# A six-layer cross network on one core: x0's first rows in three transfers, turned tile by tile; bias products with 128 rows; another order of ACT's last y

## The chip, the cores and the metric

The kernel runs on one core of a Trainium2 chip. The metric is the device time of one execution in microseconds. Engines are named as in the profile: PE (TensorE), DVE (VectorE), ACT (ScalarE), POOL (GpSimd), SP (SyncE, which here only issues DMAs).

## The reference

```python
B, F, D, L = 4096, 26, 16, 6
Din = min(F * D, 1024)            # 416
# x0 (B, Din), ws (L, Din, Din), bs (L, Din), all bfloat16
def reference(x0, ws, bs):
    x = x0
    for l in range(ws.shape[0]):
        x = x0 * (x @ ws[l] + bs[l]) + x
    return x
```

## The kernel before

The kernel works on x transposed: columns of x are partitions, rows of x run along the free axis. The 416 columns are three chunks c (or k, as the contracted side) of 128 and a tail of 32. The 4096 rows are four pairs p of two blocks of 512 rows. Since x stays a product with x0, only t = x @ w + (running sum of the biases) is kept in PSUM: PSUM accumulates over the layers of one pair, and each layer's x is (PSUM + cb) * x0, where `cb_sb` holds the running sums of the biases plus one. One step n = p * 6 + l is one layer of one pair, 24 in all.

A step on PE is `main(p, l, 0, n)` (block 0, chunks m = 0 to 2), `tail(p, l, n)` (the tail's share, four row groups side by side, and the tail's own output in `ps_tail`), and `main(p, l, 1, n)`. Each of the five results (tail products, tail output, chunks 0 to 2 of block 1) raises `s_pe`. DVE answers with six scalar_tensor_tensor per step (`s_dve`): chunk 0 of block 0, the tail, chunk 1 of block 0, chunks 0 to 2 of block 1. ACT and POOL make chunk 2 of block 0 together (L702, L289), and ACT copies the tail's halves into each other's partitions (L666).

In the first step block 0 is done by `first()` instead. x0's first 512 rows come as rows into `xin_sb` (four tiles j of 128 rows), PE transposes them into PSUM (L320) against `ident`, and DVE copies them to `x0T_sb` (L579), raising `s_ev`. Chunk 0 is copied in two halves (j 0 to 1, j 2 to 3, in different PSUM banks), chunks 1 and 2 in one piece each. Then three groups of products follow, for k = 0, 1, 2 (L348, shown as L380, the helper's line); group k waits for its weights `s_w0[k]` and for `s_ev` >= k + 2. Between k = 0 and k = 1 PE transposes the tail of both blocks (L352) from `xtn_sb`, which POOL puts together from `xin_sb` and `xtb_sb` (L260), and makes the running sums of the biases with four products (L331): `bsa_sb` (a row of ones and six rows of biases) and `bs4_sb` (the tail's 32 biases four times, made by POOL at L269) against the triangle `u_sb`. DVE turns these into `cb_sb` (L589); POOL then makes `cl_sb` (L279).

Step 0's `tail` waits for `s_ev` 5 (the tail of x0), `s_cb`, `s_w30` (the tail rows of layer 0's weights, `w3_sb`, spread from 32 to 128 partitions by two ACT copies, L674), `s_dup` (the tail's halves swapped by DVE, L587) and `s_wc0` (the corner of the weights, four POOL copies, L276).

Ahead of all that PE runs 28 products of constants, `idle(28)` (L308), whose results are not used.

Issue order of the DMAs at the start. SP's queue: x0 rows 0 to 255, three weight chunks of layer 0 (L165), a transposing DMA for block 1 (L168), then, after a wait for the last of the three weights, the weights of layers 1 to 5 (L173, L177). ACT's queue: x0 rows 256 to 511 (L643), the 32 tail columns of block 1 (`xtb_sb`, L646), the biases (L649), the tail rows of layer 0's weights (L650). Behind these on ACT stand the load of its table and a dummy activation (L653).

The last step (n = 23) is done the other way round by `last()`: the outputs are rows, so that no transpose is needed. Eight row tiles j get three products each with x as the stationary side (`rows`, L489), the tail's products (L551), and the sum so far, y, added in by products with the identity (`add_y`, L498). y is PSUM plus `cl_sb`, copied by ACT in `sums` (L681) after step 22 in the order of a list of (block, chunk, steps of DVE to wait for), each raising `s_y`; chunk 3 is the tail's `yt_sb`. DVE makes one y too (L621, `s_yd`). `rows(j)` waits for `s_y` at 2, 3, 3, 4 for j = 0 to 3, L551 for `s_y` 6 and `s_yd`. In step 22's `main` of block 1, chunk 2, the second half waits for `s_y` 1, as its bank also holds the tail that ACT reads. DVE (L630, L636) and ACT with POOL (L723, L297) then multiply by x0's rows, and SP and ACT send the tiles out.

Of the kernel before, what the change touches and what calls it, by code (L numbers as in the profile page):

```python
# [11 lines left out]
def bass_standalone__dcn_v2_cross__recsys_kernel(  # L12
# [13 lines left out]
    B, D = x0.shape  # L26
    L = ws.shape[0]
    DF = 384
    DR = D - DF
    assert DR == 32  # L30
    NB = 512
# [8 lines left out]
    with ExitStack() as es:  # L40
# [25 lines left out]
        ones_sb = sb("ones_sb", [128, 128])  # L66
        bsa_sb = sb("bsa_sb", [L + 1, D])
        bs4_sb = sb("bs4_sb", [L + 1, 4, DR])
        u_sb = sb("u_sb", [L + 1, L])
        cb_sb = sb("cb_sb", [128, 4, L], FP32)  # L70
# [28 lines left out]
        def sem(name):  # L99
            return es.enter_context(nc.semaphore(name))  # L100
# [6 lines left out]
        s_w = [sem("s_w%d" % i) for i in range(L)]  # L107
        s_xin = [sem("s_xin%d" % i) for i in range(2)]
        s_xtb, s_xtp, s_inT, s_ev = sem("s_xtb"), sem("s_xtp"), sem("s_inT"), sem("s_ev")
# [43 lines left out]

        DH = D // 2
        MADE = ((2, 0, D), (3, 0, DH))
# [3 lines left out]
        def _(sp):  # L159

            sp.dma_start(
                xin_sb[:, 0:2, :], x0[0:256, :].rearrange("(j b) d -> b j d", b=128)
            ).then_inc(s_xin[0], 16)
            for k in range(3):
                sp.dma_start(  # L165
                    w_sb[:, 0, k, :], ws[0, k * 128:(k + 1) * 128, :]
                ).then_inc(s_w0[k], 16)
# [75 lines left out]
        def _(pool):  # L243
            pool.memset(ones_sb[:, :], 1.0).then_inc(s_ones, 1)
            pool.memset(bsa_sb[0:1, :], 1.0).then_inc(s_setup, 1)
            pool.wait_ge(s_ones, 1)
# [4 lines left out]
            pool.affine_select(  # L251
                out=u_sb[:, :], in_=ones_sb[0:L + 1, 0:L], pattern=[[1, L]],
                compare_op=ALU.is_ge, fill=0.0, base=1, channel_multiplier=-1,
# [3 lines left out]
            for h, src in enumerate((xin_sb[:, :, DF:D], xtb_sb[:, :, :])):  # L257
# [11 lines left out]
            pool.tensor_copy(  # L269
                out=bs4_sb[:, :, :], in_=bsa_sb[:, DF:D].unsqueeze(1).broadcast_to([L + 1, 4, DR])  # L270
            ).then_inc(s_bs4, 1)
# [31 lines left out]
        def _(pe):  # L303
# [5 lines left out]

            idle(28)  # L310
            pe.wait_ge(s_setup, 3)
# [3 lines left out]

            def turn(c):
                for j in range(4):
                    if c == 0 and j % 2 == 0:
                        pe.wait_ge(s_xin[j // 2], 16)
                    ins = pe.transpose(  # L320
                        out=psT[:, at(c, j), j * 128:(j + 1) * 128],
                        in_=xin_sb[:, j, c * 128:(c + 1) * 128], identity=ident[:, :],
                    )
                    if c == 0 and j == 1:
                        ins.then_inc(s_inT, 1)
                ins.then_inc(s_inT, 1)

# [11 lines left out]
            def first():  # L339

                for c in range(3):
                    turn(c)
                for k in range(3):
# [5 lines left out]
                    if k == 0:  # L349
                        pe.wait_ge(s_xtp, 2)  # L350
                        for c in range(2):
                            ins = pe.transpose(  # L352
                                out=psT[:, 2, c * 128:(c + 1) * 128],
                                in_=xtn_sb[:, 0, c, :], identity=ident[:, :],
                            )
                        ins.then_inc(s_inT, 1)
                        biases()

# [37 lines left out]
            def main(p, l, blk, n):  # L396
                for m in range(3):
# [12 lines left out]
                    if blk == 1 and m == 2 and n == N1 - 1:  # L410

                        for h in range(2):
                            if h == 1:
                                pe.wait_ge(s_y, 1)
                            for k in range(3):
# [21 lines left out]
            def tail(p, l, n):  # L437
                if n == 0:
                    pe.wait_ge(s_ev, 5)
                    pe.wait_ge(s_cb, 1)  # L440
                    pe.wait_ge(s_w30, 2)
                    pe.wait_ge(s_wt[0], 16)
# [133 lines left out]
        def _(dve):  # L576
# [9 lines left out]
            for o, i in swapped(x0t_sb[:, 0]):  # L586
                dve.tensor_copy(out=o, in_=i).then_inc(s_dup, 1)  # L587
            dve.wait_ge(s_inT, 6)
            dve.tensor_copy(  # L589
# [52 lines left out]
        def _(act):  # L642
            act.dma_start(  # L643
                xin_sb[:, 2:4, :], x0[256:512, :].rearrange("(j b) d -> b j d", b=128)
            ).then_inc(s_xin[1], 16)
            act.dma_start(  # L646
                xtb_sb[:, :, :], x0[NB:2 * NB, DF:D].rearrange("(j b) d -> b j d", b=128)
            ).then_inc(s_xtb, 16)
            act.dma_start(bsa_sb[1:L + 1, :], bs[:, :]).then_inc(s_bs, 16)  # L649
            act.dma_start(w3_sb[0:DR, 0, :], ws[0, DF:D, :]).then_inc(s_wt[0], 16)  # L650

# [17 lines left out]
            act.wait_ge(s_wt[0], 16)  # L669
            for i in range(2):  # L670
                r = DR << i
                if i:
                    act.wait_ge(s_w30, i)
                act.activation(  # L674
                    out=w3_sb[r:2 * r, 0, :], in_=w3_sb[0:r, 0, :], func=ACTF.Copy
                ).then_inc(s_w30, 1)

            def sums(n):
# [6 lines left out]
                act.wait_ge(s_cl, 1)  # L685
                for blk, c, d in ((0, 3, 2), (0, 0, 2), (0, 2, 2), (0, 1, 3), (1, 0, 4), (1, 1, 5)):
                    act.wait_ge(s_dve, DV * n + d)
# [72 lines left out]
```

## Time and profile before

| what | value |
|---|---|
| time, median of 3 runs | 129.14 us (129.0 to 129.2) |
| time of the profiled execution | 129.91 us |
| its span, first to last instruction | 128.1 us |
| PE busy | 124.6 us, 97% of the span |
| DVE / ACT / POOL busy | 93.2 / 45.3 / 32.0 us |
| chain that ended last | PE 95%, DVE 3% |
| granted clock over the span | 1.00 |

All times in the text come from the profiled execution and count from its first instruction. PE is also shown as PEld, its weight loads, which overlap its products; a product's duration includes some 0.2 us of draining, while the next one starts in the meantime, so the spacing of starts tells the pace. A DMA's time to landing counts from the start of its issue.

### The profile page before, as it was taken

Reading aid. Unit: us, or ns where it says so; the run is one execution under the profiler, and the core shown is the slowest. Engines: PE = TensorE matmul, PEld = TensorE weight load, DVE = VectorE, ACT = ScalarE, POOL = GpSimd, SP = SyncE. Lnnn points to the kernel's source line nnn. Section 1 sums busy time; section 2 is a strip of 40 time slices with the busy share of each in tenths; the row PEclk is TensorE's granted clock in tenths of the full one; section 3 lists DMA queues with packets and bytes.
Section 4 is the critical chain, followed back from the end, with each engine's and each line's share of the span. In section 5 each row is a group of like instructions: output and inputs, shape, how many; then the busy total and the mean of one; then the engine's idle time right before and its main releaser. Section 6 shows DMA issues by size and latency. Waiting matters only on the chain.

```text
span 128.1 us, 5809 instructions
## 1 busy us (share of the span) xinstructions
PE 124.6 (97%) x2931; PEld 66.3 (52%) x2403; DVE 93.2 (73%) x155; ACT 45.3 (35%) x99; POOL 32.0 (25%) x42
## 2 busy tenths in 40 slices
PE   7999999999999999999999999999999999999991
PEld 7654554555445545545545545545545545545571
DVE  0449669669669669679678688697696696696873
ACT  0435436436404314214314224224224134134820
POOL 5323303303303213213123023033033033033040
PEclk9999999999999999999999999999999999999999
DMA  3979999397399700697100987000000758000017
GB/s 97 265 167 299 199 126 158 52 109 157 75 284 71 146 12 15 131 121 237 35 15 10 96 160 262 9 0 5 0 15 15 139 112 266 5 5 0 0 49 222
DMA packets 35624, 13.27 MB, mean 104 GB/s; under 512 B 26987, under 2 KB 35601, under 8 KB 35601
## 3 DMA queue, kind: packets, MB, share of 16 engines
q1 hardware_dynamic: 33912, 12.07, 49.0%
q10 hardware_dynamic: 1688, 0.83, 2.4%
q8 instruction: 21, 0.34, 1.2%
q14 instruction: 3, 0.02, 0.0%
HBM read 3.99 MB, written 3.41 MB: 58 GB/s over the span
## 4 chain that ended last, share of the span: by engine, by line
PE 95%; DVE 3%; DVEq 0%; issue 0%
PE ps L390 61%; PE ps L370 11%; PE ps L457 8%; PE ps L478 6%; PE ps L380 4%; PE ps L308 2%; DVE o_sb L630 2%; PE ps L320 1%; PE ps L551 0%; DVE o_sb L636 0%; PE ps L352 0%; PE ps L331 0%; DVEq L40 0%; DVEq L627 0%
## 5 line engine op out<-in xcount | busy, mean ns | idle before, releaser
L601 DVE SCALAR_TENSOR_TENSOR xT_sb<-ps,cb_sb,x0T_sb 128x512 bf16<-128x512 f32 x100 | 69.4, 744 | 22.3 <-PE ps L457 22.3
L390 PE MATMUL ps<-xT_sb,w_sb 128*32 128x512 bf16 (+1 forms) x1380 | 75.7, 343 | 0.0
L390 PEld LDWEIGHTS ps<-xT_sb,w_sb 128*32 128x32 bf16 x1380 | 37.0, 97 | 35.2 <-issue 8.1
L289 POOL TENSOR_TENSOR xT_sb<-t_sb,x0T_sb 128x512 bf16<-128x512 f32 x20 | 23.2, 1162 | 72.3 <-ACT t_sb L702 72.3
L702 ACT ACTIVATE t_sb<-ps,cb_sb 128x512 f32<-128x512 f32 x23 | 15.8, 687 | 61.1 <-PE ps L457 61.1
L370 PE MATMUL ps<-xT_sb,w_sb 128*32 128x256 bf16 x444 | 26.6, 273 | 0.0
L666 ACT ACTIVATE xt_sb<-xt_sb 64x256 bf16<-64x256 bf16 x38 | 15.8, 415 | 9.8 <-DVE xt_sb L610 9.3
L390 PE MATMUL ps<-x0T_sb,w_sb 128*32 128x512 bf16 (+1 forms) x252 | 14.1, 344 | 0.0
L601 DVE SCALAR_TENSOR_TENSOR xo_sb<-ps,cb_sb,x0T_sb 128x512 bf16<-128x512 f32 x15 | 10.4, 744 | 3.3 <-PE ps L457 3.3
L390 PEld LDWEIGHTS ps<-x0T_sb,w_sb 128*32 128x32 bf16 x252 | 6.7, 97 | 6.5 <-issue 1.5
L457 PE MATMUL ps<-xt_sb,w_sb 32*128 32x256 bf16 x228 | 9.6, 271 | 0.0
L478 PE MATMUL ps<-xT_sb,w_sb 128*32 128x256 bf16 x228 | 9.5, 273 | 0.0
L610 DVE SCALAR_TENSOR_TENSOR xt_sb<-ps,cb_sb,x0t_sb 128x256 bf16<-128x256 f32 x20 | 9.5, 475 | 0.0
L457 PEld LDWEIGHTS ps<-xt_sb,w_sb 32*128 32x128 bf16 x228 | 4.2, 92 | 6.2 <-issue 6.1
L289 POOL TENSOR_TENSOR xo_sb<-t_sb,x0T_sb 128x512 bf16<-128x512 f32 x3 | 3.5, 1163 | 11.2 <-ACT t_sb L702 11.2
L478 PEld LDWEIGHTS ps<-xT_sb,w_sb 128*32 128x32 bf16 x228 | 6.1, 97 | 0.1
L390 PE MATMUL ps<-xt_sb,wc_sb 128*32 128x256 bf16 x76 | 5.6, 283 | 0.0
L380 PE MATMUL ps<-w_sb,xT_sb 128*128 128x416 bf16 (+2 forms) x27 | 5.2, 320 | 0.0
L370 PE MATMUL ps<-x0T_sb,w_sb 128*32 128x256 bf16 x84 | 5.0, 273 | 0.0
L660 ACT ACTIVATE wc_sb<-w_sb 32x32 bf16<-32x32 bf16 x20 | 4.5, 226 | 0.5
L579 DVE COPY x0T_sb<-ps 128x256 bf16<-128x256 bf16 (+1 forms) x4 | 1.4, 358 | 4.5 <-PE ps L320 4.4
L390 PEld LDWEIGHTS ps<-xt_sb,wc_sb 128*32 128x32 bf16 x76 | 1.9, 92 | 4.0 <-issue 4.0
(54 smaller groups left out, 51.3 us busy)
## 6 DMA issues: line engine op xcount, KB each, us to landing
out_dram<-o_sb SPq DMA_DIRECT2D x3, 832.0 KB, 4.2
w_sb<-in_ws_dram SPq DMA_DIRECT2D x5, 312.0 KB, 5.3
xr_sb<-in_x_dram SPq DMA_DIRECT2D x1, 832.0 KB, 6.2
w_sb<-in_ws_dram SPq DMA_DIRECT2D x5, 104.0 KB, 3.4
out_dram<-o_sb SPq DMA_DIRECT2D x2, 208.0 KB, 2.1
w_sb<-in_ws_dram ACTq DMA_DIRECT2D x3, 104.0 KB
xin_sb<-in_x_dram SPq DMA_DIRECT2D x1, 208.0 KB, 3.1
xin_sb<-in_x_dram ACTq DMA_DIRECT2D x1, 208.0 KB, 3.3
```

What stands on the lines that cost most here:

```text
L289: pool.tensor_tensor(out=xdst(p, l, 0, 2), in0=t_sb[:, n % 2, :], in1=x0c(p, 0, 2), op=ALU.mult,).then_inc(s_pl, 1)
L308: pe.matmul(ps[:, 0, 0:128], lhsT=ones, rhs=ones, start=True, stop=True)
L370: return pe.add_instruction(mybir.InstMatmult(name="I-%d" % (1000000 + count[0]), engine=mybir.EngineType.PE, start_tensor_calc=start, sto ...
L380: return pe.matmul(out, lhsT=lhsT, rhs=rhs, start=start, stop=stop, skip_group_check=True)
L390: ins = pe.matmul(out[c:c + 32, :], lhsT=lhsT[:, c:c + 32], rhs=rhs, start=start, stop=stop, skip_group_check=True, tile_position=(0, c),)
L457: ins = pe.matmul(part(blk, m, h ^ other), lhsT=w3_sb[32 * g:32 * g + 32, l, m * 128:(m + 1) * 128], rhs=xt[32 * g:32 * g + 32, other, :], ...
L478: ins = pe.matmul(ps_tail[32 * g:32 * g + 32, :], lhsT=w_sb[:, l, k, DF:D], rhs=xsrc(p, l, g % 2, k)[:, (g // 2) * NT:(g // 2 + 1) * NT], ...
L601: dve.scalar_tensor_tensor(out=halves(xdst(p, l, blk, c)), in0=chunk2(blk, c), scalar=cb_sb[:, c, l:l + 1], in1=halves(x0c(p, blk, c)), op ...
L610: dve.scalar_tensor_tensor(out=tdst(p, l), in0=ps_tail, scalar=cb_sb[:, 3, l:l + 1], in1=x0t_sb[:, p, 0, :], op0=ALU.add, op1=ALU.mult,).t ...
L660: act.activation(out=wc_sb[gs, l, gs], in_=w3_sb[gs, l, DF:D], func=ACTF.Copy).then_inc(s_wc, 1)
L666: act.activation(out=o, in_=i, func=ACTF.Copy).then_inc(s_dup, 1)
L702: act.activation(out=halves(t_sb[:, n % 2, :]), in_=chunk2(0, 2), func=ACTF.Identity, bias=cb_sb[:, 2, l:l + 1],).then_inc(s_act, 1)
```

## The change

- x0's first 512 rows come in three transfers: tile 0 (SP's first), tile 1 (ACT's first), tiles 2 and 3 (SP's second). Layer 0's first weight chunk goes to ACT's queue as its second; SP keeps the other two. On ACT the tail weights go ahead of the biases, and the biases wait for the memset of `bsa_sb`.
- PE transposes all three chunks of tile 0, then of tile 1, then tiles 2 and 3 chunk by chunk. 23 filler products instead of 28.
- The bias products take 128 rows: `bsa_sb`, `bs4_sb` and `u_sb` have 128 partitions (ones, and zeros in `u_sb` below row 6), and the products come between k = 1 and k = 2.
- The second copy that spreads `w3_sb` is split: ACT takes the left half of the columns, DVE the right half, ahead of its copy of the bias sums. `tail` waits for three copies.
- ACT's y for chunk 0 of block 0 comes first, after DVE's first step, and the tail's second; PE's wait in step 22 is for two y.

```diff
--- before.py
+++ after.py
@@ -27,6 +27,7 @@
     L = ws.shape[0]
     DF = 384
     DR = D - DF
+    DH = D // 2
     assert DR == 32
     NB = 512
     NP = B // (2 * NB)
@@ -64,9 +65,10 @@
         act_sb = sb("act_sb", [128, 1], FP32)
         ident = sb("ident", [128, 128])
         ones_sb = sb("ones_sb", [128, 128])
-        bsa_sb = sb("bsa_sb", [L + 1, D])
-        bs4_sb = sb("bs4_sb", [L + 1, 4, DR])
-        u_sb = sb("u_sb", [L + 1, L])
+
+        bsa_sb = sb("bsa_sb", [128, D])
+        bs4_sb = sb("bs4_sb", [128, 4, DR])
+        u_sb = sb("u_sb", [128, L])
         cb_sb = sb("cb_sb", [128, 4, L], FP32)
         ps = es.enter_context(nc.psum_tensor("ps", [128, 8, NB], FP32))
         psT = ps.bitcast(BF16)
@@ -105,7 +107,7 @@
         s_wt = [sem("s_wt%d" % i) for i in range(L)]
         s_w0 = [sem("s_w0_%d" % i) for i in range(3)]
         s_w = [sem("s_w%d" % i) for i in range(L)]
-        s_xin = [sem("s_xin%d" % i) for i in range(2)]
+        s_xin = [sem("s_xin%d" % i) for i in range(3)]
         s_xtb, s_xtp, s_inT, s_ev = sem("s_xtb"), sem("s_xtp"), sem("s_inT"), sem("s_ev")
         s_x0 = [sem("s_x0_%d" % i) for i in range(NP)]
         s_tn = [sem("s_tn%d" % i) for i in range(NP)]
@@ -151,17 +153,17 @@
 
         DB = D - (NB - D)
 
-        DH = D // 2
         MADE = ((2, 0, D), (3, 0, DH))
         SPLIT = ((ps[:, 7, 0:DB], 0, DB), (ps[:, 6, D:NB], DB, D))
 
         @block.sync
         def _(sp):
 
+            sp.dma_start(xin_sb[:, 0, :], x0[0:128, :]).then_inc(s_xin[0], 16)
             sp.dma_start(
-                xin_sb[:, 0:2, :], x0[0:256, :].rearrange("(j b) d -> b j d", b=128)
-            ).then_inc(s_xin[0], 16)
-            for k in range(3):
+                xin_sb[:, 2:4, :], x0[256:512, :].rearrange("(j b) d -> b j d", b=128)
+            ).then_inc(s_xin[2], 16)
+            for k in (1, 2):
                 sp.dma_start(
                     w_sb[:, 0, k, :], ws[0, k * 128:(k + 1) * 128, :]
                 ).then_inc(s_w0[k], 16)
@@ -242,14 +244,14 @@
         @block.gpsimd
         def _(pool):
             pool.memset(ones_sb[:, :], 1.0).then_inc(s_ones, 1)
-            pool.memset(bsa_sb[0:1, :], 1.0).then_inc(s_setup, 1)
+            pool.memset(bsa_sb[:, :], 1.0).then_inc(s_setup, 1)
             pool.wait_ge(s_ones, 1)
             pool.affine_select(
                 out=ident[:, :], in_=ones_sb[:, :], pattern=[[-1, 128]],
                 compare_op=ALU.is_equal, fill=0.0, base=0, channel_multiplier=1,
             ).then_inc(s_setup, 1)
             pool.affine_select(
-                out=u_sb[:, :], in_=ones_sb[0:L + 1, 0:L], pattern=[[1, L]],
+                out=u_sb[:, :], in_=ones_sb[:, 0:L], pattern=[[1, L]],
                 compare_op=ALU.is_ge, fill=0.0, base=1, channel_multiplier=-1,
             ).then_inc(s_setup, 1)
             pool.memset(wc_sb[:, :, :], 0.0).then_inc(s_g, 1)
@@ -267,7 +269,7 @@
             pool.wait_ge(s_bs, 16)
             pool.wait_ge(s_setup, 1)
             pool.tensor_copy(
-                out=bs4_sb[:, :, :], in_=bsa_sb[:, DF:D].unsqueeze(1).broadcast_to([L + 1, 4, DR])
+                out=bs4_sb[:, :, :], in_=bsa_sb[:, DF:D].unsqueeze(1).broadcast_to([128, 4, DR])
             ).then_inc(s_bs4, 1)
             pool.wait_ge(s_g, 1)
             pool.wait_ge(s_wt[0], 16)
@@ -307,23 +309,25 @@
                 for _ in range(n):
                     pe.matmul(ps[:, 0, 0:128], lhsT=ones, rhs=ones, start=True, stop=True)
 
-            idle(28)
+            idle(23)
             pe.wait_ge(s_setup, 3)
             def at(c, j):
 
                 return 4 if (c, j // 2) == (0, 1) else (2, 3, 6)[c]
 
-            def turn(c):
-                for j in range(4):
-                    if c == 0 and j % 2 == 0:
-                        pe.wait_ge(s_xin[j // 2], 16)
+            def turns():
+
+                order = [(j, c) for j in range(2) for c in range(3)]
+                order += [(j, c) for c in range(3) for j in range(2, 4)]
+                for j, c in order:
+                    if c == 0 and j < 3:
+                        pe.wait_ge(s_xin[j], 16)
                     ins = pe.transpose(
                         out=psT[:, at(c, j), j * 128:(j + 1) * 128],
                         in_=xin_sb[:, j, c * 128:(c + 1) * 128], identity=ident[:, :],
                     )
-                    if c == 0 and j == 1:
+                    if (j, c) == (1, 0) or j == 3:
                         ins.then_inc(s_inT, 1)
-                ins.then_inc(s_inT, 1)
 
             def biases():
                 pe.wait_ge(s_bs4, 1)
@@ -338,8 +342,7 @@
 
             def first():
 
-                for c in range(3):
-                    turn(c)
+                turns()
                 for k in range(3):
                     pe.wait_ge(s_w0[k], 16)
                     pe.wait_ge(s_ev, k + 2)
@@ -354,6 +357,7 @@
                                 in_=xtn_sb[:, 0, c, :], identity=ident[:, :],
                             )
                         ins.then_inc(s_inT, 1)
+                    elif k == 1:
                         biases()
 
             def pieces(blk, m, x):
@@ -411,7 +415,7 @@
 
                         for h in range(2):
                             if h == 1:
-                                pe.wait_ge(s_y, 1)
+                                pe.wait_ge(s_y, 2)
                             for k in range(3):
                                 o, rhs = pieces(blk, m, xsrc(p, l, blk, k))[h]
                                 ins = columns(
@@ -438,7 +442,7 @@
                 if n == 0:
                     pe.wait_ge(s_ev, 5)
                     pe.wait_ge(s_cb, 1)
-                    pe.wait_ge(s_w30, 2)
+                    pe.wait_ge(s_w30, 3)
                     pe.wait_ge(s_wt[0], 16)
                 elif l == 0:
                     pe.wait_ge(s_x0t[p], 16)
@@ -585,6 +589,10 @@
             dve.wait_ge(s_ev, 5)
             for o, i in swapped(x0t_sb[:, 0]):
                 dve.tensor_copy(out=o, in_=i).then_inc(s_dup, 1)
+            dve.wait_ge(s_w30, 1)
+            dve.tensor_copy(
+                out=w3_sb[64:128, 0, DH:D], in_=w3_sb[0:64, 0, DH:D]
+            ).then_inc(s_w30, 1)
             dve.wait_ge(s_inT, 6)
             dve.tensor_copy(
                 out=cb_sb[:, :, :],
@@ -640,14 +648,14 @@
 
         @block.scalar
         def _(act):
-            act.dma_start(
-                xin_sb[:, 2:4, :], x0[256:512, :].rearrange("(j b) d -> b j d", b=128)
-            ).then_inc(s_xin[1], 16)
+            act.dma_start(xin_sb[:, 1, :], x0[128:256, :]).then_inc(s_xin[1], 16)
+            act.dma_start(w_sb[:, 0, 0, :], ws[0, 0:128, :]).then_inc(s_w0[0], 16)
             act.dma_start(
                 xtb_sb[:, :, :], x0[NB:2 * NB, DF:D].rearrange("(j b) d -> b j d", b=128)
             ).then_inc(s_xtb, 16)
+            act.dma_start(w3_sb[0:DR, 0, :], ws[0, DF:D, :]).then_inc(s_wt[0], 16)
+            act.wait_ge(s_setup, 1)
             act.dma_start(bsa_sb[1:L + 1, :], bs[:, :]).then_inc(s_bs, 16)
-            act.dma_start(w3_sb[0:DR, 0, :], ws[0, DF:D, :]).then_inc(s_wt[0], 16)
 
             act.wait_ge(s_ones, 1)
             act.activation(out=act_sb[:, :], in_=ones_sb[:, 0:1], func=ACTF.Identity)
@@ -667,13 +675,13 @@
 
 
             act.wait_ge(s_wt[0], 16)
-            for i in range(2):
-                r = DR << i
-                if i:
-                    act.wait_ge(s_w30, i)
-                act.activation(
-                    out=w3_sb[r:2 * r, 0, :], in_=w3_sb[0:r, 0, :], func=ACTF.Copy
-                ).then_inc(s_w30, 1)
+            act.activation(
+                out=w3_sb[DR:2 * DR, 0, :], in_=w3_sb[0:DR, 0, :], func=ACTF.Copy
+            ).then_inc(s_w30, 1)
+            act.wait_ge(s_w30, 1)
+            act.activation(
+                out=w3_sb[64:128, 0, 0:DH], in_=w3_sb[0:64, 0, 0:DH], func=ACTF.Copy
+            ).then_inc(s_w30, 1)
 
             def sums(n):
 
@@ -683,7 +691,7 @@
                     ).then_inc(s_y, 1)
 
                 act.wait_ge(s_cl, 1)
-                for blk, c, d in ((0, 3, 2), (0, 0, 2), (0, 2, 2), (0, 1, 3), (1, 0, 4), (1, 1, 5)):
+                for blk, c, d in ((0, 0, 1), (0, 3, 2), (0, 2, 2), (0, 1, 3), (1, 0, 4), (1, 1, 5)):
                     act.wait_ge(s_dve, DV * n + d)
                     if c == 3:
                         y(yt_sb[:, :], ps_tail, 3)

```

## The prediction

> **What bounds the kernel now.** The page comes first: TensorE (PE) holds 95% of the chain that ended last and is 97% busy, and from 9.51 us on its steps repeat every 4.89 us (L390's long pieces start at 9.51, 14.40, 19.29), so only what PE does before the first of them and after the last can move. I therefore read the chain of waits over the first 9.6 us.
>
> ```profile
> 0.83 3.14 PE ps L308 x28
> 3.97 0.03 issue
> 4.00 1.44 PE ps L320 x12
> 5.44 1.28 PE ps L380 x4
> 6.72 0.21 PE ps L352 x2
> 6.93 0.18 PE ps L331 x4
> 7.11 1.41 PE ps L380 x8
> 8.52 0.44 PE ps L457 x12
> ```
>
> It shows filler (L308), 12 transposes (L320), layer 0's products for k=0 (L380 x4), two tail transposes (L352), the bias products (L331), then k=1 and k=2 (L380 x8) and the tail (L457). Four products took 1.28 us, the next eight 1.41: PE runs at half pace until about 6.8 us, although the clock column says 1.00 throughout. At half pace 128 columns take 107 ns (1.28 us over 1536 columns), at full pace some 55. The chain's starts lie up to 0.2 us behind the timeline's where results drain; by the timeline the first transpose starts at 4.00, k=0 at 5.23, k=1 at 7.04 and the tail at 8.45.
>
> Next the transfers that this waits for. DMA issues, with size and us to landing:
>
> ```profile
> xin_sb<-in_x_dram SPq DMA_DIRECT2D x1, 208.0 KB, 3.1
> xin_sb<-in_x_dram ACTq DMA_DIRECT2D x1, 208.0 KB, 3.3
> ```
>
> Layer 0's weights by their line, and the first stretches by windows (last figure GB/s):
>
> ```profile
> L165 SPq DMA_DIRECT2D w_sb<-in_ws_dram x3: 425/432/447, 1.3 to 2.3; - x3
> ...
> DMA to landing us min/median/max: 3.3/3.4/3.7
> ```
>
> ```profile
> 1.80:2.60 0.80, 0.80 (x11) 0.80 (x9) 0.00 (x0) 0.00 (x0) 0.72 (x2) 1.00 0.73 128
> 2.60:3.40 0.80, 0.80 (x10) 0.80 (x9) 0.00 (x0) 0.50 (x1) 0.00 (x0) 1.00 1.07 354
> ```
>
> Both halves of x0 are issued at 0.79 and land at 3.9 and 4.1; the three weights of layer 0 (issued at 1.31, 1.81, 2.27) at 4.6, 5.2 and 6.0. The first transpose answers the first landing. From 2.6 us on the DMA engines are full, so a transfer moved forward pushes another back.
>
> Last, the timeline of the end.
>
> ```profile
> 117.81 0.47 ACT L681 ACTIVATE yt_sb<-ps,cl_sb 128x256 bf16<-128x256 f32 x1 [0.55 <-DVE xt_sb L610]
> 118.19 2.99 ACT L681 ACTIVATE y_sb<-ps,cl_sb 128x512 bf16<-128x512 f32 x5
> ...
> 119.01 2.27 PE L380 MATMUL ps<-w_sb,xT_sb 128*128 128x416 bf16 x12
> ...
> 120.27 0.74 DVE L621 TENSOR_SCALAR y_sb<-ps,cl_sb 128x512 bf16<-128x512 f32 x1
> 121.25 0.13 PEld L551 LDWEIGHTS ps<-w_sb,xt_sb 32*128 32x128 bf16 x4 [0.38 <-issue]
> 121.28 0.36 PE L551 MATMUL ps<-w_sb,xt_sb 32*128 32x416 bf16 x4
> ```
>
> ACT's six y run until 121.18 and L551 starts just behind. The 12 row products, 176 ns apart, were issued by 121.12.
>
> **The base.** The profiled execution took 129.91 us: 128.1 of span and 1.8 around it. It is 0.77 above the median of 129.14. I work out differences on the profile's rows and put them on the median.
>
> **Transfers and transposes.** SP's queue held 208 KB of x0 and then 104 KB of weights; it will hold 104 KB (tile 0) and then 208 KB (tiles 2 and 3). ACT's held 208 KB and 32 KB; it will hold tile 1, the k=0 weights and those 32 KB. So the end of tiles 2 and 3 stands after 312 KB of SP's queue with 208 KB of large rows beside it, the place of the first weights before: 4.6 us. The other bound is 4.1: if the three x0 transfers finish ahead of the weights, they are the same 416 KB as before. I take 4.55, nearest to the first row, as two queues of equal load have shared the engines about evenly here. Tiles 0 and 1 are 208 KB; 102 KB had moved by 2.6 us, the rest takes 0.3 us at 354 GB/s, and the 416 KB landed 0.6 us after such a reckoning (3.5 against 4.1), so both are there by about 3.5, tile 0 at 3.2 to 3.5. Filler of 23 ends at 0.83 + 23 x 0.107 = 3.29 (five products, 0.53 us, go), and six transposes (0.64 us) fit before 4.2. That takes 0.64 us of work off what follows the last landing, but PE then waits 0.4 us for it.
>
> After that landing (T) the way to k=0 is not the six transposes (T + 0.69) but the copy of chunk 0: 0.05 for the wait, 0.45 from the first of two transposes to DVE's copy (4.00 to 4.41 in the timeline, plus 0.05 as these two stand 0.107 apart), 0.29 for a 256-wide copy, 0.13 back to PE (3.86 to 4.00 at the first landing): T + 0.92. k=0 thus starts at 5.47, where it started at 5.23. The weights for k=0 (now about 4.1) cover it; k=1 (5.2) and k=2 (6.0) keep their places in SP's queue.
>
> **Layer 0 and the biases.** k=0 at half pace: 5.47 to 6.75. The tail transposes run across the change of pace, 0.15: 6.90. k=1: four products at full pace 0.655 (eight from 7.04 to 8.36): 7.56. The old bias products took 0.32, from 6.73 to 7.05; four products of 6 columns 26 ns apart are 0.1 of it, and the rest is PE running empty around the 7-row form (weight load idle 0.20). With 128 rows that goes. The trace has no such product: its bounds are 4 x 26 ns = 0.10 and 4 x 56 ns = 0.22 (128-row products with new weights at L380 near the end), and I take 0.18, as every one loads new weights. A saving of 0.14, of 0.22 at the low bound. The Trainium skill (TensorE: Matmul & The Clock Gate, LDWEIGHTS) says that a weight load's time goes by columns and not by rows; this alone would give the low bound, and the loads here (92 ns for 7 rows, 98 for 128) lean that way. Then 7.74, k=2 to 8.40, 0.10 before the tail: 8.49 against 8.45, so **+0.04**.
>
> **What is covered.** ACT's issues become five: w3 leaves at about 2.3 (before 2.5), still behind xtb, and lands by 6.0; the biases go last, at 2.6, and land near 6.1 (before 5.5). The wait ahead of them is for the memset, done by 1.4; only ACT's table load (1.28) and a dummy activation stand behind it, done by 4.7, and ACT's next work waits for w3 anyway. POOL waits for three x landings, copies xtn twice (0.29 each, until 5.1; needed at 6.75), then bs4 by 6.5 (needed 7.56) and wc by 7.5 (needed 8.9). Each copy costs its own delay once that slack, 1 us or more, is gone. The w3 copies: ACT 0.55 and about 0.37, done by 7.0; DVE's part (0.22, like the 64x256 copies) stands ahead of its copy of the bias sums. DVE: x0t at 7.15, two copies until 7.9, w3 until 8.1, bias sums until 8.25, and PE needs them at 8.4. That cover is only 0.1 us, and the one that I trust least. The larger memset and select on POOL end by 2.6 as now (same length per row).
>
> **The end.** ACT's first y can start when DVE's first step is done (117.33) and not its second: at 117.42. At 0.57 apart the last ends at 120.8, not 121.18. L551 then waits for DVE's y (until 121.01) and for the row products (121.12), and starts about 121.22: **-0.05**, which DVE's last outputs pass on. PE's wait for two y instead of one is met at 118.47, with the products behind it due at 118.52: nothing, or up to 0.1 that the row products' own wait (118.9) takes in.
>
> **Sum:** +0.04 - 0.05, about zero: 129.1 us. With T from 4.4 to 4.7 and the biases at either bound the sum goes from -0.2 to +0.15: 128.95 to 129.3.
>
> **Rivals.** *The x rows land at 4.1 (faster).* k=0 from 5.03 to 6.31, transposes to 6.52, k=1 partly at half pace to 7.3, biases 0.1 to 0.18, k=2, tail at 8.2 to 8.25: -0.2 to -0.25, with the end -0.25 to -0.3: 128.85. For it: SP's queue sends first and ACT's landed 0.2 later. Against it: equal shares. 0.28.
>
> *The pace doubles one stretch later (slower).* Two stretches as the trace has them, PE's busy time first:
>
> ```profile
> 0.00:3.40 3.40, 2.57 (x25) 2.60 (x26) 0.00 (x0) 0.50 (x1) 1.87 (x9) 1.00 0.42 113
> 3.40:6.80 3.40, 3.37 (x24) 2.23 (x21) 1.35 (x4) 1.70 (x4) 1.39 (x6) 1.00 1.07 241
> ```
>
> After 2.57 of 3.40 us PE stayed at half pace; after 3.37 it went to full. This count includes some 0.2 us of drain behind a product (a transpose shows 0.31 for its 0.107). The new start has a hole from 4.2 to 4.6 and one of 0.2 before k=0; drained, some 0.3 to 0.4 us of them stay empty: 3.0 of 3.4 (88%), between the two. If that is too little and the next 3.4 us run at half pace, they hold 1.7 us less work: 130.8. It decides as soon as the hole counts. The Trainium skill (TensorE: Matmul & The Clock Gate, Part 1) describes this as a clock gate that opens after one busy window of about 3.4 us and warns of DMA waits; the trace agrees with the length, and no row shows how busy is enough. 0.30.
>
> *The bias sums come late* because w3 or x0 landed 0.3 to 0.5 later than reckoned: +0.3 to +0.5, 129.5. 0.08.
>
> **Numbers.** The forecast has 0.34. A difference under 0.2% (0.26 us) can't be told from none here. Of the forecast's 0.34, 0.23 stays within that, 0.07 is faster, 0.04 slower; of the early landing 0.25 faster, 0.03 the same; the other two, 0.38, are slower. Faster 0.32, same 0.26, slower 0.42. The forecast's own range is 128.95 to 129.3; the whole runs from 128.8 to 130.9, as leaving the late clock out would leave out 3 in 10.
>
> **What would show it.** Tiles 2 and 3 landing near 4.55, k=0 at 5.47, no empty weight load around the biases, the tail at 8.5, and ACT's last y done by 120.8, with the row products and DVE's y the last before L551. It is wrong if the change of pace moves, if k=0 starts by 5.1, or if the tail waits for DVE.

## The result: 0.3% slower, and the profile after

The changed kernel takes 129.52 us in the median (129.23 to 131.51, 17 runs) beside 129.10 (128.76 to 129.78, 17 runs) for the kernel before: a ratio of 1.0032 [1.0017, 1.0046], or +0.2 to +0.6 us. Three of the 17 runs of the changed kernel, at 131.3 to 131.5, lie apart from the others (129.23 to 129.91) and are not in the ratio. The forecast was no change: 129.1 us, with a range of 128.95 to 129.3. The profiled execution of the changed kernel took 129.34, with a span of 127.5: it is shorter than the profiled execution before (129.91, 128.1), while the medians say the opposite. That contradiction is the key to the case.

The chain of waits of the changed kernel over its first 9.6 us (start, length, what):

```profile
1.25 3.15 DMA xin_sb<-in_x_dram
4.39 0.05 issue
4.44 0.82 PE ps L325 x6
5.26 0.05 issue
5.31 1.18 PE ps L384 x4
6.49 0.11 PE ps L355 x2
6.60 0.65 PE ps L384 x4
7.25 0.08 PE ps L335 x4
...
8.00 0.50 PE ps L461 x12
```

The chain used to begin in the filler; now it hangs on a transfer. Tiles 2 and 3, issued at 1.25, land at 4.39, their six transposes (L325) follow, and k=0 (L384) starts at 5.31, 0.92 after the landing. Four products take 1.18 us, the next four 0.65: the pace doubles inside k=0, at about 6.1 by the spacing of the starts (0.42 us at first, 0.22 in k=1). In the profile before it doubled between the tail transposes, 0.106 us apart, and the bias products at 6.86. The tail starts at 7.99 instead of 8.45.

The transfers of x0's rows in the changed kernel (size, us to landing), and POOL's second copy of the tail rows:

```profile
xin_sb<-in_x_dram SPq DMA_DIRECT2D x1, 208.0 KB, 3.1
...
xin_sb<-in_x_dram SPq DMA_DIRECT2D x1, 104.0 KB, 2.4
xin_sb<-in_x_dram ACTq DMA_DIRECT2D x1, 104.0 KB, 2.6
```

```profile
5.75 0.29 POOL L262 COPY xtn_sb<-xtb_sb 128x128 bf16<-128x128 bf16 x1 [0.90 <-DMA xtb_sb<-in_x_dram]
```

Tiles 0 and 1 land at 3.2 and 3.4, tiles 2 and 3 at 4.39, where the last rows used to land at 4.13. `xtb_sb` lands at 5.7, where it used to land at 4.75, and POOL's copy from it ends at 6.04: here just ahead of the tail transposes at 6.32, because k=0 ran mostly at half pace.

The timeline of the end:

```profile
116.96 0.69 ACT L689 ACTIVATE y_sb<-ps,cl_sb 128x512 bf16<-128x512 f32 x1 [0.16 <-DVE xT_sb L609]
...
117.91 2.42 ACT L689 ACTIVATE y_sb<-ps,cl_sb 128x512 bf16<-128x512 f32 x4
...
118.51 2.28 PE L384 MATMUL ps<-w_sb,xT_sb 128*128 128x416 bf16 x12
...
120.73 0.35 PE L555 MATMUL ps<-w_sb,xt_sb 32*128 32x416 bf16 x4
```

ACT's last y ends at 120.33, well ahead of L555. From the first row product to L555 it is 2.22 us, where it was 2.27 (119.01 to 121.28). From the start of step 0's tail to the end of the span it is 119.51 us (127.5 less 7.99, with the third decimals of the trace), where it was 119.60.

### The profile page after: what moved, and what is told of

It is laid out like the page before. It is cut to its first block, busy times and chain, and to the rows that moved or that the text cites. A ratio compares the mean times of both kernels' runs of the same rounds, so it can differ in the third digit from the quotient of the medians.

```text
span 127.5 us, 5800 instructions
## 1 busy us (share of the span) xinstructions
PE 123.6 (97%) x2925; PEld 65.5 (51%) x2398; DVE 93.4 (73%) x156; ACT 45.1 (35%) x99; POOL 32.0 (25%) x42
## 4 chain that ended last, share of the span: by engine, by line
PE 92%; DVE 3%; DMA 2%; SPq 0%; issue 0%; DVEq 0%
PE ps L394 62%; PE ps L374 11%; PE ps L461 8%; PE ps L482 6%; PE ps L384 4%; DMA xin_sb<-in_x_dram 2%; DVE o_sb L638 2%; PE ps L325 1%; PE ps L555 0%; DVE o_sb L644 0%; SPq L162 0%; DVEq L41 0%; PE ps L355 0%; PE ps L335 0%; DVEq L635 0%
## 5 line engine op out<-in xcount | busy, mean ns | idle before, releaser
L384 PE MATMUL ps<-w_sb,xT_sb 128*128 128x416 bf16 (+2 forms) x27 | 5.2, 320 | 0.0
```

What stands on the lines that cost most here:

```text
L384: return pe.matmul(out, lhsT=lhsT, rhs=rhs, start=start, stop=stop, skip_group_check=True)
```

## What was to be told apart

The theory after the result: the profile before was not typical. In most runs the pace doubles much earlier; then nothing of what the change takes off PE's early path counts, while what it adds to the landings counts in full. The rivals: the hole in PE's work ahead of tiles 2 and 3 costs time in every run (the pace doubles later), and the reordered end or the 128-row biases cost time.

Three kinds of kernel answer this. "Held back" kernels (h_, g_) make SP and ACT wait for a large memset on POOL before the first DMA, with more filler ahead, so that PE is at full pace when the rows land. Kernels without filler (c_) keep PE at half pace until into k=2. The others (u_) start as the kernel does. In all held-back kernels the wait adds some 7 us, so they are compared only with each other. The runs fall into batches, in which the kernel before has medians of 129.09 to 129.41 us; a difference of less than some 0.3 us between kernels of different batches (h_before and h_after stand in one, h_xtb and h_w0 in another, h_rest and h_by in a third) is therefore read from the profiles and not from the medians.

## Held back with narrow filler: too much else moved

```diff
+        go_sb = sb("go_sb", [128, 7000])
+            pool.memset(go_sb[:, :], 0.0).then_inc(s_go, 1)   # after the memset of wc_sb
+            sp.wait_ge(s_go, 1)                               # ahead of SP's first DMA
+            act.wait_ge(s_go, 1)                              # ahead of ACT's first DMA
-            idle(28)
+            idle(140)                                         # 130 in g_after, g_xtb
```

g_before is the kernel before so held back, g_after the changed one. g_rest is the changed kernel with the transfers, turns and loads of before. g_xtb is g_after with `xtb_sb` issued ahead of the k=0 weights.

> The kernel before, with all its start DMAs held back until POOL has done a long memset (some 8.4 us more) and 140 filler products in that time, so that PE is at full pace before the first row lands. Base for the next three; its own expectation: the time of before plus some 8 us, with PE at full pace from the first transpose (55 ns apart, not 107) and k=0 about 0.8 us after the second x landing, not 1.1. Both theories say the same here.

> The changed kernel, held back in the same way (130 fillers). Theory pace: the change costs where PE is already at full pace, as k=0 then hangs on the last x landing plus 0.9 us, and that landing is 0.3 us later: 0.2 to 0.3 us slower than g_before. Theory hole: the change costs only by the hole in PE's work that puts the doubling of the pace off; with the pace full beforehand it must come out 0.1 to 0.2 us faster than g_before (biases, y). Theory rest: y, biases or the split copy cost it, then g_rest shows the same loss.

> The changed kernel with the transfers, the order of transposes and the loads of before, held back in the same way: only the bias products with 128 rows between k=1 and k=2, the split w3 copy, the biases' late issue and ACT's y order are left. Theory pace and theory hole: 0.05 to 0.2 us faster than g_before. Theory rest: 0.2 us or more slower than g_before.

> g_after with xtb (32 KB) issued ahead of the k=0 weights on ACT's queue. xtb landed at 5.7 in the changed kernel, where it was 4.8 before. If at full pace the tail transposes wait for it, this is 0.1 to 0.2 us faster than g_after, with the tail transposes right behind k=0. If the last x landing alone decides, it is the same, or slower by what the small rows take from x's landing (up to 0.2 us).

Measured: g_before 137.33 us (136.38 to 137.69, 4 runs), g_after 139.00 (138.34 to 139.20), g_rest 136.53 (136.36 to 137.11), g_xtb 137.61 (137.30 to 138.00). The order is as the theory has it, g_after the slowest and g_rest the fastest, but the sizes are several times those expected (1.67 us between g_before and g_after, not 0.2 to 0.3), and they can't be used. The DMA view of g_before from 7 to 14 us shows one reason:

```profile
q8 instruction: 1, 0.02, 1.0%
```

One packet of 16 KB of instructions takes 1.0% of 16 engines over 7 us, that is 1.1 us of one DMA engine, and it falls at 8.0 to 8.6 us, on the first transfers (issued at 8.41). The second issue on ACT's queue took 1.22 us in g_before and 0.77 in g_after, where the issues beside them take 0.41 to 0.48. Tiles 2 and 3 of g_after landed 4.04 us after the start of their issue, against 3.15 in the chain above. In g_rest the packet came at 7.29, ahead of the transfers. The other reason is that the loss of g_after doesn't lie at the start at all: step 0's tail starts at 16.06 in g_before and at 16.05 in g_after, and from there to the end it is 119.74 and 121.33 us. In that stretch PE of g_after stands empty from 24.36 to 25.31, for nothing that the profile shows. So these four kernels say little on what the change costs at the start.

## Held back with wide filler: the whole loss, at full pace

```diff
-            idle(28)
+            idle(35)     # 33 in h_after; each product now 512 columns wide
```

Fewer filler products of 512 columns keep PE as busy, and in the profiles the instruction packet stays clear of the first transfers (it comes at 16.43 in h_before and at 17.57 in h_after).

> The kernel before, held back by POOL's memset as in g_before, but with 35 filler products of 512 columns instead of 140 of 128, so that PE has fetched as many instructions as ever by then: in g_before a fetch of 16 KB ran beside the first transfers. Some 8 us above before; the two x landings 3.1 and 3.3 us after their issue as in before, k=0 0.8 us behind the second, runs within 0.5 us of each other.

> The changed kernel held back in the same way with 33 fillers of 512 columns. At full pace throughout. Theory late landing: the last x landing 3.6 us after the first issue, where h_before has 3.35, k=0 0.2 to 0.3 us later than h_before's and the time 0.1 to 0.3 us longer. Theory hole: k=0 no later and the time 0.1 to 0.2 us shorter, since no change of pace is left to put off. If it is 1.5 us longer again, the fetch was not what stretched g_after.

Measured: h_before 136.36 us (136.25 to 136.41), h_after 137.00 (136.79, 136.92, 137.08 and 138.72). The profiled executions took 136.41 and 136.79. PE's timeline of h_before, then of h_after, then POOL's of h_after:

```profile
12.51 0.81 PE L385 MATMUL ps<-x0T_sb,w_sb 128*128 128x512 bf16 x4
13.15 0.28 PE L357 MATMUL ps<-ident,xtn_sb 128*128 128x128 bf16 x2
13.36 0.22 PE L336 MATMUL ps<-u_sb,bsa_sb 7*128 7x6 bf16 x3
...
13.54 1.47 PE L385 MATMUL ps<-x0T_sb,w_sb 128*128 128x512 bf16 x8
14.95 0.51 PE L462 MATMUL ps<-x0t_sb,w_sb 32*128 32x256 bf16 x12
```

```profile
12.81 0.81 PE L389 MATMUL ps<-x0T_sb,w_sb 128*128 128x512 bf16 x4 [0.25 <-DVE x0T_sb L588]
13.74 0.28 PE L360 MATMUL ps<-ident,xtn_sb 128*128 128x128 bf16 x2
13.87 0.81 PE L389 MATMUL ps<-x0T_sb,w_sb 128*128 128x512 bf16 x4
14.52 0.22 PE L340 MATMUL ps<-u_sb,bsa_sb 128*128 128x6 bf16 x3
...
14.62 0.81 PE L389 MATMUL ps<-x0T_sb,w_sb 128*128 128x512 bf16 x4
15.42 0.29 PE L466 MATMUL ps<-x0t_sb,w_sb 32*128 32x256 bf16 x4
```

```profile
13.40 0.29 POOL L266 COPY xtn_sb<-xtb_sb 128x128 bf16<-128x128 bf16 x1 [0.94 <-DMA xtb_sb<-in_x_dram]
```

The tail starts at 15.42 instead of 14.95, +0.47, and four pieces make it up. k=0 starts 0.30 later, since tiles 2 and 3 land at 12.01 and the last rows of h_before at 11.68. The tail transposes start 0.93 after k=0 instead of 0.64: 0.28 of waiting for POOL's copy, as `xtb_sb` lands at 13.35 instead of 12.21. The biases, from the end of the work ahead to the start of the work behind, take 0.11 instead of 0.28: -0.17. And the tail waits some 0.05 longer, for the table of bias sums (copied by 15.32). Together 0.30 + 0.28 - 0.17 + 0.05 = 0.46. The end then gives back 0.09 (119.51 from the tail to the end of the span, against 119.60): +0.38, as the profiled times have it (136.79 less 136.41). The medians lie 0.64 apart, with one long run among the four of h_after. The change as timed, not held back, lost 0.42.

## Without filler: the same change costs next to nothing at half pace

```diff
-            idle(28)     # c_before; idle(23) in c_after
+            idle(0)
```

> The kernel before without its filler products, so that PE has done nothing by the first landing and stays at half pace through the transposes and k=0, and mostly beyond. Base for c_after: some 0.5 to 1.7 us above before, spread over the phase at which the pace doubles; k=0 1.1 us after the second x landing.

> The changed kernel without filler products. Theory pace (at half pace PE's ten transposes after the landing cost before as much as the later landing costs now): within 0.3 us of c_before, k=0 0.9 us after the last x landing. If it is 0.5 us or more slower than c_before, as h_after is against h_before, the pace does not matter to what the change costs.

Measured: c_before 131.91 us (131.83 to 131.95, 5 runs), c_after 131.77 (131.14 to 132.57, 7 runs). The totals can't be compared: in c_before, whose PE program is 28 products shorter, a 16 KB instruction packet falls at 124.68 us into the last outputs (2.8% of 16 engines over 3 us, 1.3 us of one engine), and L551 to the end takes 7.65 us instead of 6.78 in the kernel before; in c_after one falls at 124.47, and the same stretch takes 6.98. So I read the start. The chains of c_before and of c_after:

```profile
5.36 1.28 PE ps L380 x4
...
7.05 2.29 PE ps L380 x8
9.33 0.32 PE ps L457 x5
```

```profile
5.35 1.44 PE ps L384 x4
...
9.52 0.21 PE ps L461
```

At half pace k=0 needs 1.28 us and more, and `xtb_sb` is there before it ends: the tail transposes don't wait. By the timeline k=0 starts at 5.16 and 5.35, as the last rows land at 4.06 and 4.44: of a landing 0.38 later, 0.19 is left. The tail starts at 9.27 and 9.45, 4.11 and 4.10 after k=0. In between, the bias products take 0.15 us instead of 0.33, and the change of pace, which came 0.42 later in c_after (9.22 against 8.80), costs half of 0.42. Without that shift the tails would stand within 0.03 of each other: at half pace the transfers cost 0.19, the biases give 0.18 back, and the change as a whole loses next to nothing, where it loses 0.47 at full pace, ahead of the end's 0.09.

## Parts of the change

**The rest without the transfers.** u_rest is the changed kernel with the transfers, turns, loads and 28 fillers of before; h_rest is the same, held back.

```diff
-            sp.dma_start(xin_sb[:, 0, :], x0[0:128, :]).then_inc(s_xin[0], 16)
+            sp.dma_start(
+                xin_sb[:, 0:2, :], x0[0:256, :].rearrange("(j b) d -> b j d", b=128)
+            ).then_inc(s_xin[0], 16)
...
-            idle(23)
+            idle(28)     # h_rest: 35 wide ones
```

> The changed kernel with the transfers, the order of transposes, the loads and the 28 fillers of before; nothing is held back. Only the bias products, the split w3 copy, the biases' late issue and ACT's y order are left of the change. Theory transfers (the new transfers and transposes alone make it slower, the rest gains a little): 0.1 to 0.3 us faster than before, 128.8 to 129.0. Theory rest (biases, split copy or y cost it): 129.4 to 129.6, as slow as the changed kernel. What the transfers cost in the changed kernel is then its 129.5 less this.

> u_rest (the change without its transfers, order of transposes and loads) held back with 35 wide fillers like h_before. Theory transfers: below h_before's 136.36 by 0.1 to 0.25 us (0.1 at the biases, 0.1 at the end), so that the transfers alone cost 0.8 us at full pace. Theory rest: at 136.5 or above, as the biases now land last and their products wait for them.

Measured: u_rest 128.83 us (128.55 to 130.33, 12 runs), ratio 0.9989 [0.9959, 1.0019], which doesn't tell it from the kernel before; h_rest 136.30 (136.12 to 136.46), 0.06 under h_before. Both times the transfers with their turns are what costs: the full change stands 0.69 above u_rest (129.52 less 128.83) and 0.70 above h_rest (137.00 less 136.30). In h_rest the biases, now the last of ACT's transfers, land late, as its waits say (who waited, for whom, us):

```profile
PEld ps L337 <- POOL bs_sb L274: 0.3, 1, 0.3
```

So what 128 rows save at the biases is given back in that order of ACT's issues.

**The rows of the biases and y alone.** u_by is the kernel before with 128 rows for the biases, in their old place, and the new order of y; h_by the same, held back.

```diff
-        bsa_sb = sb("bsa_sb", [L + 1, D])      # bs4_sb, u_sb alike
+        bsa_sb = sb("bsa_sb", [128, D])
+            act.wait_ge(s_setup, 1)            # ahead of the DMA of bs
-                for blk, c, d in ((0, 3, 2), (0, 0, 2), ...
+                for blk, c, d in ((0, 0, 1), (0, 3, 2), ...
```

> h_before with only the 128-row bias products, in their old place between k=0 and k=1, and ACT's y order. 0.1 to 0.25 us below h_before (136.36). If it is as fast as h_rest, place and split copy give nothing.

> The kernel before with only the 128-row bias products, in their old place, and ACT's y order; nothing held back. 0.1 to 0.3 us faster than before (128.85 to 129.0) by either theory, since neither the transfers nor the late biases are in it; no run above 130.

Measured: h_by 136.52 us (136.35 to 136.85), no gain on h_before; u_by 128.88 (128.67 to 129.42, 12 runs), ratio 0.9972 [0.9950, 0.9993]: faster than the kernel before. ACT's timeline of h_by shows where the bias saving went:

```profile
13.66 1.13 ACT L681 ACTIVATE w_sb<-w_sb 32x416 bf16<-32x416 bf16 x2 [1.62 <-DMA w_sb<-in_ws_dram]
```

`w3_sb` lands at 13.64 and its two copies last until 14.79, so the tail starts at 15.00, against 14.95 in h_before. What stays is the end: 119.50 to 119.52 us from tail to end, in every h_ and u_ kernel with the new order of y. That is 0.09 of u_by's gain; the interval (0.09 to 0.65 us) holds it, and what else there is was not taken apart. The profile of u_by has the wait of h_by too: the last product of k=2 starts at 7.12, the copies of `w3_sb` end at 7.46, and the tail starts at 7.67.

**Filler in the holes.** u_fill is the changed kernel with four fillers ahead of the transposes of tiles 2 and 3 and two ahead of k=0.

```diff
+                    if (j, c) == (2, 0):
+                        idle(4)
...
                 turns()
+                idle(2)
```

> The changed kernel with 4 filler products ahead of the transposes of tiles 2 and 3 and 2 ahead of k=0, where PE stood empty (0.52 and 0.25 us). Theory hole (PE's empty time puts the doubling of its pace off): no run near 131.4 any more, of which the changed kernel had 3 in 17, and the median at 129.1 to 129.3, as the pace doubles earlier. Theory late landing (k=0 hangs on the last landing plus 0.9 us, whatever the pace): the median stays at 129.4 to 129.6; only the long runs go.

Measured: 129.37 us (129.07 to 129.83, 12 runs), ratio 1.0026 [1.0010, 1.0041]. The median lies between the ranges of the two theories. A loss against the kernel before stays (0.13 to 0.53 us), so the usual loss is not the hole alone; but in the profile of u_fill the pace still doubled only at 6.4, so the filler did not bring the pace forward either. No run was above 129.9, where the changed kernel had 3 of 17; at 3 in 17 twelve runs would miss it with a chance of (14/17)^12 = 0.10, so that filler removes the long runs is only suggested.

**The order of the transfers.** h_xtb is h_after with `xtb_sb` ahead of the k=0 weights; h_w0 is h_after with the k=0 weights back on SP.

```diff
 h_xtb, ACT:
             act.dma_start(xin_sb[:, 1, :], ...
-            act.dma_start(w_sb[:, 0, 0, :], ...
             act.dma_start(xtb_sb[:, :, :], ...
+            act.dma_start(w_sb[:, 0, 0, :], ...
 h_w0, SP (and no w_sb on ACT):
-            for k in (1, 2):
+            for k in range(3):
```

> h_after with xtb (32 KB) issued ahead of the k=0 weights on ACT's queue. In h_after xtb landed 4.9 us after the first issue (h_before 3.8), and the tail transposes started 0.28 us after k=0's products were through. Theory xtb (that wait is half of what the change costs at full pace): xtb lands by 4.2, the tail transposes follow k=0 at once, and the time is 0.2 to 0.3 us under h_after's 137.0, unless k=0 moves. Theory x rows alone: the same 137.0.

> h_after with the k=0 weights on SP's queue behind tiles 2 and 3, as SP had them before; ACT's queue has tile 1, xtb, w3 and the biases. Theory shared queues (tiles 2 and 3 land late because the k=0 weights now run beside them): tiles 2 and 3 land 3.2 to 3.35 us after the first issue, as the 416 KB of x did in h_before, and xtb by 3.9; the k=0 weights land at about 4.3 to 4.9 and k=0 hangs on them, so the time is no better than 137.0. If tiles 2 and 3 still land at 3.6, their place in SP's queue decides and not what runs beside them.

Measured: h_xtb 137.34 us (136.77 to 138.44), h_w0 136.59 (136.32 to 136.63). The chains of the two:

```profile
9.35 3.79 DMA w_sb<-in_ws_dram
13.14 0.05 issue
13.19 0.82 PE ps L389 x4
```

```profile
8.88 2.81 DMA xin_sb<-in_x_dram
...
13.07 0.82 PE ps L389 x4
```

In h_xtb the rows land at 11.73 and `xtb_sb` at 11.92, but the weights at 13.14, and k=0 now waits for those until 13.19. In h_w0 the rows land at 11.69, as early as in h_before, `xtb_sb` at 11.85 and the weights at 13.02: k=0 at 13.07, although the rows would have allowed about 12.5 (0.80 after the landing, as in h_after). Its tail (15.39) is 0.03 ahead of h_after's, its median 0.4 below h_after's and 0.2 above h_before's, in another batch; I had expected no better than 137.0. So tiles 2 and 3 land 0.3 late because the k=0 weights run beside them; whichever goes first, PE waits for the other. All u_, c_ and h_ profiles, with before and after, agree: the last of the rows land 3.11 to 3.43 us after the first issue where the k=0 weights stand behind them in the queues, and 3.58 to 3.95 where they are issued beside them (after, u_fill, c_after, h_after).

## Why the prediction was wrong

**The base failed.** I took the profiled execution of before, with its change of pace at 6.8 us, as the kernel, and put differences on the median. It was 0.77 above that median, and slower than 73 of that kernel's 75 other runs (128.69 to 129.87, 24 of them over 129.4). Two kernels that start as before does show where PE more usually stands; the chains of u_by and u_rest:

```profile
4.09 0.90 PE ps L320 x12
4.99 0.08 issue
5.07 0.81 PE ps L380 x4
```

```profile
3.98 1.06 PE ps L321 x12
5.04 0.65 PE ps L382 x4
```

Their products run at full pace from the first on; by the spacing of the transposes the pace doubled at about 4.2 and 4.7. No second profile of the kernel before was taken, so for it this is inferred: from these two, from the sum below, and from its spread, 1.2 us, against 0.16 in four runs of h_before and 0.12 in five of c_before, where PE's pace at the start is set; other held-back kernels spread more (h_by 0.50, h_after 1.9 with its long run), so the spread alone proves little. The prediction had a rival for a later change of pace and none for an earlier one, though it named a change of pace that moves as a sign of being wrong.

With full pace from about 4.5 on, the sum comes out otherwise. The twelve transposes cost before 0.67 us instead of 1.28, so the six that the change moves ahead of the landing save next to nothing. The step of the prediction that failed first is the gain at k=0, "T + 0.92" against a start that had been 1.10 after the last landing: 0.18 at half pace, as the profiles before and after have it, but 0.03 at full pace, where k=0 starts 0.83 after the last landing without the change (11.68 to 12.51 in h_before) and 0.80 after it with the change (12.01 to 12.81 in h_after). With the landings of the two profiles, 4.13 and 4.39, that is 4.96 and 5.19, +0.23. k=0 then ends at 5.84 (0.65 for four products) and POOL's copy of `xtb_sb` at 6.04; with 0.05 for the way back to PE the transposes wait 0.25. Biases -0.17, bias sums +0.05, end -0.09: +0.27, inside the measured +0.2 to +0.6.

This closes the difference, not the levels. With k=0 at 4.96, h_before's way from there to the tail (2.44 us), 119.60 from the tail to the end and 1.85 around the span, the kernel before would take 128.85 us, and the changed one 0.27 more, 129.12; the medians are 129.10 and 129.52, so 0.25 and 0.40 are left over. Some runs with a later change of pace, or landings later than 4.39 (4.74 in u_fill), would fill that. Nor was a run of the changed start seen at full pace without being held back: in both its profiles (after, u_fill) the pace doubled inside k=0. What costs time is shown, the transfers with their turns (u_rest, h_rest), and so is how they cost it at full pace (h_before, h_after); that the usual run of the changed kernel is at full pace by then is argued.

**xtb_sb was mis-placed.** This is the second step that failed. "POOL ... copies xtn twice (0.29 each, until 5.1; needed at 6.75)" was its cover, 1 us or more. The copy ended at 6.04. `xtb_sb` now leaves third on ACT's queue instead of second, at 1.71 instead of 1.30, and lands at 5.69 instead of 4.75; I had given every other moved transfer a new landing, and this one its old one. At half pace the cover held (6.04 against 6.32); at full pace it is gone, 0.28 us in h_after.

**Right by the rows.** Tiles 0 and 1 by 3.5: 3.19 and 3.36. Tiles 2 and 3 between 4.1 and 4.6: 4.39, where I took 4.55; from profile to profile it moves (4.43 in c_after, and 4.74 in u_fill, beyond both bounds). k=0 at T + 0.92 at half pace: 5.31 after 4.39. The k=0 weights at 4.1: 4.21 in the profile after, 5.12 in u_fill. The Trainium skill (DMA: Bandwidth & Descriptors, Issuing engines are not separate DMA queues) says that transfers issued from several engines interleave on the same DMA engines; h_w0 agrees, with the rows 0.32 earlier once the weights no longer ran beside them.

**Biases.** Taken at 0.18, they measured 0.10 to 0.11, the low bound; so the rule of the Trainium skill on weight loads (TensorE: Matmul & The Clock Gate, LDWEIGHTS), that their time goes by columns, was the better guide. **The end** was taken at -0.05 and measured -0.09 in every h_ and u_ kernel with the new y order: 0.05 by the mechanism named (first row product to L551, 2.27 to 2.22), and 0.04 ahead of the row products (110.56 to 110.52 us after the tail's start), where none was forecast.

**The rivals.** "The x rows land at 4.1" did not happen. "The bias sums come late" cost 0.05. "The pace doubles one stretch later" is neither shown nor excluded. In the profile after the pace doubled earlier than before, and the hole was no bar: the 3.4 us ahead of it (us PE busy second) read

```profile
2.67:6.07 3.40, 3.04 (x22) 1.91 (x20) 1.26 (x4) 1.57 (x3) 0.58 (x2) 1.00 1.11 271
```

so 3.04 of 3.40 was enough, where 2.57 had not been, if the pace changes at the end of such a stretch; no run tests where the stretches begin. The three long runs, 1.9 over the others, are near its price of +1.7, and u_fill had none. But h_after and h_xtb, at full pace ahead of the landing, have one run each of the same kind (138.72, 138.44), and u_rest, without the hole, had 130.03 and 130.33. None of these was profiled; whether they are late clocks, late transfers or a stop like that of g_after, 0.94 us at 24.36, stays open.

On one base the steps nearly close: the tail is 0.46 earlier in the profile after, of which 0.37 is the pace doubling 0.74 earlier (half of it), 0.09 is left, and 0.09 comes from the end: -0.2 against the forecast's zero. From there to the +0.27 at full pace it is 0.45: 0.25 at the tail transposes, 0.15 at k=0 (0.18 against 0.03) and 0.05 at the biases (0.22 saved at the change of pace, 0.17 at full pace). The method was fit for a phase at the slow edge of that kernel's runs.

## What to carry to other kernels

Compare a profiled execution with the spread of the timed runs before building on it: one that lies outside may hold a phase, here the change of PE's pace, that most runs don't have, and a gain that lives on that phase isn't there in the median. Work the sum once with the phase early and once late; if the sign differs, neither is the forecast. And when a transfer moves forward, follow every transfer behind it on that queue, the smallest too, to the work that waits for it.

## What the runs showed of the hardware

- PE's change of pace moves between profiled runs of near-equal starts: about 4.2 us (u_by), 4.7 (u_rest), 6.8 (before), and 6.1 and 6.4 (after, u_fill). The Trainium skill (TensorE: Matmul & The Clock Gate, Part 1) calls the window free-running, so that the number of slow products differs between runs of one kernel; the traces agree as far as kernels with like starts can show it, as none was profiled twice, and a shift of 2.6 us is worth up to 1.3 us here (an estimate: half of it).
- A 16 KB instruction packet takes one DMA engine 1.1 to 1.3 us. Where it fell on the first transfers, issues of 0.41 to 0.48 took up to 0.77 (g_after) and 1.22 us (g_before), and a landing 4.04 instead of 3.15; in g_xtb, with a packet at 8.09, the issues took 0.51 and 0.52 and the rows landed after 2.81, so the packet is the likely cause and not a shown one. In c_before, 28 products shorter, one fell on the last outputs, and L551 to the end took 0.87 us longer.
